# Series of products on constants in row groups, ahead of the first logits of an agent attention and SoLU kernel

## The chip, the cores and the metric

The kernel runs on one core of a Trainium2 chip. The metric is the device time of one execution in microseconds (us); lower is better. The engines are TensorE (PE, with its weight loads shown apart as PEld), VectorE (DVE), ScalarE (ACT), GpSimd (POOL) and SyncE (SP), which here only issues DMAs. Each engine runs its own list of instructions in order; semaphores tie the lists together.

## The reference

Four batches of 12608 tokens with 128 channels go through an attention over 49 agents, and the result through a feed-forward part of width 1024.

```python
def sm(a, b):
    s = scale * (a @ b.transpose(0, 2, 1))
    s = s - s.max(-1, keepdims=True)
    e = np.exp(s)
    return e / (e.sum(-1, keepdims=True) + 1e-09)
agent_v = sm(agents, k) @ v
x = (sm(q, agents) @ agent_v).reshape(B * S, D)

h = x @ w_in
e = np.exp(h - np.max(h, axis=-1, keepdims=True))
solu = h * (e / (np.sum(e, axis=-1, keepdims=True) + 1e-09))
ln = (solu - mean) / np.sqrt(var + 1e-06) * g_ln
out = ln @ w_out
```

## The kernel before

Phase A (`phase_a`) computes `agent_v` for a batch and folds it with `w_in`. The keys come in 12 chunks of 1024 and a tail: logits of a chunk on PE (`p1_mm`, L523, two products of 512 columns into the two halves of the output partitions), a running maximum on DVE (L528, L533 and L535), the exponential on ACT (L549), transposes on PE (`p2_t`, L556), a copy out of PSUM (L567), products with v on PE (`p2_mm`, L577) and their accumulation on DVE (L586). For batch 0, the head of the kernel, the chunks of k and v are loaded ahead into buffers that the later phases use (`kload` L501, `vload` L512, both on SP's queue; the second four slabs of v take the buffers of the first four of k). Beside this DVE, ACT and POOL convert the weights, which arrive as 64-bit numbers, to float32 (`pair_f64`, L368). The head ends with the folded matrices `mh` and `ml` (L648, L653), computed from L641.

Phase B makes the softmax over the agents for 8 tiles of 128 tokens at a time (L767 to L817). Phase C does the feed-forward part of the 396 tiles: L867 (products into the two-bank tiles `ph2`), L871 (maximum), L881 (exponential), L886, L892, then for one half of the tiles transposes on PE (L899) and fp32r products (L982), for the other half a transpose on DVE (L906), DMAs (L916) and float32 products (L922).

The order of all this is set before the kernel runs. `Plan` simulates the engines with costs and due times and emits the instructions in the order in which they would start; at the end each engine's instructions from `marks` (L469) on are tied to that order. What was emitted before `marks`, the constants, is placed by the scheduler where it fits: `ident` (L330, made by POOL), `identR`, its fp32r copy by DVE (L332), `ones` (L334, DVE), and the zeroed `packs` (L453, POOL). Where the plan sees PE idle for over 0.2 us before the head's end, `idle` (L1068) fills in products on `ones` into `ph2[1]` (L1071), 14 of them at the start. They are part of PE's fixed list. The PSUM tiles are `ph2`, two of two banks each, and four banks `px`.

```python
def idle(gap):
    if mlast[0].end is None and gap > 0.2:
        for _ in range(int(0.7 * gap / 0.11) if plan.at["P"] > 2.0 else 14):
            nc.tensor.matmul(ph2[1][:, : 2 * P], warm[:, :P], warm, start=True, stop=True)
```

Of the kernel before, what the change touches and what calls it, by code (L numbers as in the profile page):

```python
# [25 lines left out]
class Plan:  # L26
# [28 lines left out]
    def op(self, eng, fn, cost, due, deps=(), take=False, free=None, after=(), kind=1, shy=0.0):  # L55
        o = Op()
        o.kind, o.shy = kind, shy
        o.eng, o.fn, o.cost, o.due, o.take, o.free = eng, fn, cost, due, take, free
        o.deps, o.outs, o.end, o.bank = [d for d in deps if d is not None], [], None, None
        o.left = 0  # L60
        for d in o.deps + [d for d in after if d is not None]:
            if d.end is None:
                o.left += 1
                d.outs.append(o)
        if not o.left:
            self.push(o)
        return o
# [133 lines left out]
def kernel(  # L201
# [11 lines left out]
    nc = tc.nc  # L213
# [3 lines left out]
    P = 128  # L217
    NF = DF // P
    HW = 512
# [109 lines left out]
    ident = const.tile([P, P], F32, name="ident")  # L329
    make_identity(nc, ident)  # L330
    identR = const.tile([P, P], F32R, name="identR")
    nc.vector.tensor_copy(out=identR, in_=ident)  # L332
    ones = const.tile([P, P], F32, name="ones")
# [116 lines left out]
    packs = []  # L450
# [13 lines left out]
    ph2 = [ps_h.tile([P, DF], F32, name=f"ph{i}") for i in range(2)]  # L464
# [2 lines left out]
    plan.HOLD, plan.STICK = HLD, STK  # L467
    op = plan.op
    marks = len(nc.cur_bb.bb.instructions)  # L469

    TB = NCK * CT + (CKT + P - 1) // P
    seq = [(b, t) for b in range(B) for t in range(TB)]
# [639 lines left out]
    for x in range(n):  # L1112
        b, t = seq[x]
        G, j = slot[x]
        i = x // 2
# [14 lines left out]
        if isY:  # L1130
            TBT[x] = op("D", F(c_tb, x), 1.165, at(x, DTB, DTBR, DTBL), [U[x]] + MV.get(back(G, 2), []))
            if j == GT - 1:
                a = [TBT[2 * z + q] for z in units[G][1] for q in range(2)]
# [4 lines left out]
                for q in range(GT * NF // YC):  # L1138
                    a, k0 = divmod(q * YC, NF)
# [42 lines left out]
        if j == GT - 1:  # L1182
# [21 lines left out]
            else:  # L1204
                o = op("D", d0, 0.6, x + DR, [o, SP[utl[-UTB]]])
                p = op("P", d1, 0.88, x + DR, [o], take=True)
# [71 lines left out]
```

## Time and profile before

| | us |
|---|---|
| time, median of 3 runs | 1471.67 |
| lowest and highest run | 1469.97, 1474.09 |
| span of the profiled execution, first to last instruction | 1472.9 |
| PE busy | 1444.4 |
| DVE busy | 1376.2 |
| ACT busy | 1291.1 |
| POOL busy | 1071.1 |

The profile was taken of one execution of the same program; its span stands within the spread of the runs, 1.2 us above their median, and no other time is given for it. Busy times are sums over an engine's instructions. The matmuls of PE are pipelined, so that one row's duration is longer than the distance to the next one; where a pace is wanted, the starts of neighbours count. A releaser is what ended an idle time, found from the semaphores.

### The profile page before, as it was taken

The numbers are of one execution on the slowest core, as the hardware profiler recorded it, in microseconds if no ns is written. First come the engines' busy times: TensorE is split into PE (matmuls) and PEld (weight loads), VectorE is DVE, ScalarE is ACT, GpSimd is POOL, SyncE is SP. The second block draws the span as 40 slices with busy tenths as digits, with TensorE's granted clock in tenths as the row PEclk, the third lists the DMA queues.
The fourth block names the chain that finished last, engine by engine and source line by source line (L and its number), as shares of the span: only waits on it lengthen the run. The fifth ranks groups of instructions, "written<-read, shape, count | busy, mean of one in ns | idle before, by whom it ended". The sixth has DMA issues, their size and how long they took to land.

```text
span 1472.9 us, 33358 instructions
## 1 busy us (share of the span) xinstructions
PE 1444.4 (98%) x12033; PEld 1279.7 (87%) x12033; DVE 1376.2 (93%) x2024; ACT 1291.1 (88%) x2486; POOL 1071.1 (73%) x1521
## 2 busy tenths in 40 slices
PE   8889999999999999999999999999999999999998
PEld 4668889898888898899898798998999999999998
DVE  5899999999999999999989899999999999999985
ACT  5489999999898998899987898988989999999985
POOL 2485887777776777688677667787768887887854
PEclk9899999999999999999999999999999999999999
DMA  9356565565456756654746666566455455554541
GB/s 369 130 137 194 145 166 149 152 160 142 130 140 187 183 144 160 155 167 114 191 105 159 175 169 175 142 164 166 113 140 135 116 150 131 132 142 106 138 107 44
DMA packets 113253, 221.90 MB, mean 151 GB/s; under 512 B 47552, under 2 KB 50880, under 8 KB 113088
## 3 DMA queue, kind: packets, MB, share of 16 engines
q1 hardware_dynamic: 113088, 219.77, 55.7%
q8 instruction: 95, 1.56, 0.5%
q14 instruction: 70, 0.57, 0.1%
HBM read 92.87 MB, written 26.15 MB: 81 GB/s over the span
## 4 chain that ended last, share of the span: by engine, by line
PE 64%; DVE 15%; ACT 12%; issue 4%; DMA 3%; SPq 2%; POOL 0%; ACTq 0%; DVEq 0%; POOLq 0%
PE ph L867 16%; PE px L922 16%; PE px L982 13%; PE px L899 8%; DVE u L886 5%; ACT e L881 5%; DVE nm L871 4%; ACT uT L952 3%; ACT e L892 3%; PE px L523 3%; DVE tb L906 3%; PE px L577 3%; PE px L767 2%; SPq L916 2%; PE px L812 1%
## 5 line engine op out<-in xcount | busy, mean ns | idle before, releaser
L881 ACT ACTIVATE e<-ph,nm 128x1024 f32<-128x1024 f32 x396 | 443.3, 1123 | 88.1 <-DVE nm L871 84.4
L871 DVE TENSOR_REDUCE nm<-ph 128x1 f32<-128x1024 f32 x396 | 467.2, 1207 | 31.8 <-PE ph L867 29.9
L886 DVE SCALAR_TENSOR_TENSOR u<-ph,e 128x1024 f32<-128x1024 f32 x396 | 471.7, 1218 | 18.7 <-ACT e L881 15.1
L965 POOL TENSOR_TENSOR uL<-uT,uH 128x1024 fp32r<-128x1024 f32 (+1 forms) x198 | 471.3, 2380 | 12.2
L892 ACT ACTIVATE e<-u,su 128x1024 bf16<-128x1024 f32 x396 | 459.1, 1163 | 20.2 <-DVE u L886 19.6
L922 PE MATMUL px<-w,uY 128*128 128x128 f32 x3072 | 375.6, 276 | 0.0
L922 PEld LDWEIGHTS px<-w,uY 128*128 128x128 f32 x3072 | 359.9, 192 | 13.9 <-issue 8.4
L867 PE MATMUL ph<-mh,pT 128*128 128x512 f32 x792 | 335.4, 423 | 7.7 <-DVE u L886 7.3
L867 PE MATMUL ph<-ml,pT 128*128 128x512 f32 x792 | 312.8, 395 | 1.9 <-DVE ml L653 1.9
L961 POOL TENSOR_SCALAR uH<-uT 128x1024 fp32r<-128x1024 f32 (+1 forms) x198 | 207.8, 1049 | 87.0 <-ACT uT L952 87.0
L982 PE MATMUL px<-uH,wH 128*128 128x256 f32 x816 | 237.8, 291 | 0.4 <-ACT eT L567 0.4
L906 DVE STREAM_TRANSPOSE tb<-u 128x1024 f32<-128x1024 f32 x192 | 235.8, 1233 | 0.7
L982 PE MATMUL px<-uH,wL 128*128 128x256 f32 x816 | 228.4, 280 | 0.0
L982 PE MATMUL px<-uL,wH 128*128 128x256 f32 x816 | 228.0, 279 | 0.0
L952 ACT COPY uT<-px 128x512 f32<-128x512 f32 x394 | 213.7, 597 | 11.7 <-PE px L899 11.1
L899 PE MATMUL px<-ident,u 128*128 128x128 f32 x1632 | 218.1, 275 | 1.1 <-ACT uT L952 0.6
L899 PEld LDWEIGHTS px<-ident,u 128*128 128x128 f32 x1632 | 186.2, 142 | 15.8 <-ACT uT L952 3.8
L867 PEld LDWEIGHTS ph<-mh,pT 128*128 128x128 f32 x792 | 150.1, 190 | 39.5 <-DVE u L886 13.4
L867 PEld LDWEIGHTS ph<-ml,pT 128*128 128x128 f32 x792 | 150.7, 190 | 24.4 <-DVE ml L653 2.3
L982 PEld LDWEIGHTS px<-uH,wH 128*128 128x128 f32 x816 | 153.8, 188 | 15.6 <-issue 11.4
L982 PEld LDWEIGHTS px<-uL,wH 128*128 128x128 f32 x816 | 155.2, 190 | 3.7 <-issue 0.5
L982 PEld LDWEIGHTS px<-uH,wL 128*128 128x128 f32 x816 | 153.7, 188 | 0.0
(127 smaller groups left out, 1570.1 us busy)
## 6 DMA issues: line engine op xcount, KB each, us to landing
uY<-tb SPq DMA_DIRECT2D x768, 128.0 KB, 2.6
qt<-in_qT_dram SPq DMA_DIRECT2D x48, 512.0 KB, 4.2
kt<-in_kT_dram SPq DMA_DIRECT2D x36, 512.0 KB, 4.4
vt<-in_v_dram SPq DMA_DIRECT2D x36, 512.0 KB, 4.1
rB<-dr SPq DMA_DIRECT2D x50, 256.0 KB, 4.1
out_dram<-rB SPq DMA_DIRECT2D x50, 256.0 KB, 2.0
out_dram<-oy SPq DMA_DIRECT2D x48, 256.0 KB, 2.7
kh<-in_kT_dram SPq DMA_DIRECT2D x12, 512.0 KB, 8.7
```

The source lines that it names most:

```text
L867: nc.tensor.matmul(ph[:, sl], lhs, bmats[b]["mh" if m == 0 else "ml"][:, sl], start=(m == 0), stop=(m == 1))
L871: nc.vector.tensor_reduce(out=nms[x], in_=phs[x], op=ALU.max, axis=AX.X, negate=True)
L881: nc.scalar.activation(out=es[x], in_=phs[x], func=AF.Exp, bias=nms.pop(x), accum_out=st[G]["S"][:, j : j + 1])
L886: nc.vector.scalar_tensor_tensor(out=u, in0=phs[x], scalar=INV, in1=es[x], op0=ALU.mult, op1=ALU.mult, accum_out=su)
L892: nc.scalar.activation(out=sq, in_=u, func=AF.Square, bias=su, scale=-float(DF), accum_out=st[G]["Q"][:, j : j + 1])
L899: nc.tensor.transpose(pt[:, kf * P : (kf + 1) * P], us[x][0][:, k0 * P : (k0 + 1) * P], ident)
L906: nc.vector.transpose(to, us[x][0].rearrange("p (k r c) -> p k r c", r=GT, c=SQB))
L922: nc.tensor.matmul(st[G]["po"][:, a * P : (a + 1) * P], yb[G][1][:, a, kf].rearrange("p x c -> p (x c)"), w2[:, kf, :], start=(kf == 0), s ...
L952: nc.scalar.copy(out=rr[x][:, hf * 4 : hf * 4 + 4, :], in_=pt)
L961: nc.gpsimd.tensor_scalar(out=uH, in0=rr[x][:, k0:k1, :], scalar1=1.0, scalar2=0.0, op0=ALU.mult, op1=ALU.add)
L965: nc.gpsimd.tensor_tensor(out=uL, in0=rr[x][:, k0:k1, :], in1=uH.bitcast(F32), op=ALU.subtract)
L982: nc.tensor.matmul(po, wt[:, kf, :], ut[:, kf, :], start=(q == 0), stop=(q == WM - 1))
```

## The change

Right after `marks`, and so ahead of everything that the plan emits, PE gets seven series of products. `trial(rows, cols, steps, lhs, rhs)` cuts the 128 partitions into groups of `rows`, and in each of `steps` rounds gives every group one product of `cols` columns: the group's rows of the identity (`ident`, float32, or `identR`, fp32r) as weights and its rows of `ones` (read again for each block of 128 columns) or of the zeros in `packs[0]` as the moving operand. Each group accumulates over the rounds in one of the four banks of `ph2`. Nothing reads the results; the banks are overwritten later. The plan does not know of these products, so the order of everything else stays.

```diff
     marks = len(nc.cur_bb.bb.instructions)
+
+    def banks(q):
+        return ph2[q // 2][:, (q % 2) * HW : (q % 2 + 1) * HW]
+
+    wide = ones.unsqueeze(1)
+    zeros = packs[0].rearrange("p j i a -> p (j i a)")
+
+    def trial(rows, cols, steps, lhs, rhs):
+        m = cols // P
+        for s in range(steps):
+            for g in range(P // rows):
+                sl = slice(g * rows, (g + 1) * rows)
+                nc.tensor.matmul(banks(g)[:, :cols], lhs[sl, :], rhs(sl, m), start=(s == 0), stop=(s == steps - 1))
+
+    one = lambda sl, m: wide[sl].to_broadcast([sl.stop - sl.start, m, P])
+    rnd = lambda sl, m: zeros[sl, : m * P]
+    trial(32, 128, 12, ident, one)
+    trial(32, 256, 6, ident, one)
+    trial(32, 512, 3, ident, one)
+    trial(64, 512, 4, identR, rnd)
+    trial(32, 256, 6, identR, rnd)
+    trial(128, 512, 4, identR, rnd)
+    trial(128, 128, 8, ident, one)
```

## Rows read from the trace of the kernel before

**Rows 1.** The page: span, shares of the chain that ended last.
```profile
span 1472.9 us, 33358 instructions
...
PE 64%; DVE 15%; ACT 12%; issue 4%; DMA 3%; SPq 2%; POOL 0%; ACTq 0%; DVEq 0%; POOLq 0%
```

**Rows 2.** Timeline, 0 to 30 us: start, duration, engine, line, operation, [idle before].
```profile
1.05 3.17 PE L1071 MATMUL ph<-ones 128*128 128x256 bf16 x14 [1.05 <-DVE ones L334]
1.20 0.30 POOL masks.py:199 TENSOR_SCALAR_AFFINE_SELECT ident<-ident 128x128 f32<-128x128 f32 x1
...
1.44 0.99 POOL L453 MEMSET pack<- 128x512 f32 x2
...
5.99 4.29 PE L523 MATMUL px<-kh,ag_sb 128*64 128x512 f32 x12 [1.77 <-DMA kh<-in_kT_dram]
...
8.00 0.69 DVE L528 TENSOR_REDUCE mxp<-px 128x1 f32<-128x512 f32 x1 [7.01 <-PE px L523]
...
10.32 0.22 DVE L332 CAST identR<-ident 128x128 fp32r<-128x128 f32 x1
...
11.19 0.63 PE L556 MATMUL px<-ident,ek 128*128 128x128 f32 x4 [0.36 <-ACT ek L549]
...
11.74 1.08 PE L523 MATMUL px<-kh,ag_sb 128*64 128x512 f32 x4
```

**Rows 3.** Waits, 0 to 70 us: who waited for whom, total us, times, longest.
```profile
PE px L523 <- DMA kh<-in_kT_dram: 1.8, 1, 1.8
```

**Rows 4.** The chain that ended last, 0 to 80 us: start, duration, what.
```profile
17.96 1.01 PE px L523 x4
...
37.62 1.90 PE px L577 x16
...
42.79 1.02 PE px L577 x16
```

**Rows 5.** Timeline of PE, 0 to 60 us, columns as in group 2.
```profile
53.25 1.88 PE L641 MATMUL px<-win_sb,av_dup 128*128 128x512 f32 x4
54.97 1.25 PE L1071 MATMUL ph<-ones 128*128 128x256 bf16 x10
```

**Rows 6.** Instructions of one line (L641, L1071): duration in ns, min/median/max, first and last start.
```profile
L641 PE MATMUL px<-win_sb,av_dup x16: 590/592/697, 53.3 to 1123.4; 128*128 128x512 f32 x16
...
L1071 PE MATMUL ph<-ones x69: 269/273/421, 1.0 to 56.0; 128*128 128x256 bf16 x69
```

**Rows 7.** Timeline of PE in the steady part, 706 to 722 us.
```profile
712.32 0.28 PE L982 MATMUL px<-uH,wH 128*128 128x256 f32 x1
712.44 0.28 PE L982 MATMUL px<-uL,wH 128*128 128x256 f32 x1
...
713.82 1.95 PE L922 MATMUL px<-w,uY 128*128 128x128 f32 x16
715.74 1.53 PE L899 MATMUL px<-ident,u 128*128 128x128 f32 x12
717.02 0.47 PE L867 MATMUL ph<-mh,pT 128*128 128x512 f32 x1
717.33 0.39 PE L867 MATMUL ph<-ml,pT 128*128 128x512 f32 x1
717.56 0.40 PE L867 MATMUL ph<-mh,pT 128*128 128x512 f32 x1
...
719.04 1.14 PE L767 MATMUL px<-ag_sb,qt 128*64 128x49 f32 x32
```

**Rows 8.** Windows: stretch, busy us of each engine, granted clock, DMA share, GB/s.
```profile
0.00:2.00 2.00, 0.95 (x5) 0.71 (x6) 0.17 (x1) 0.00 (x0) 1.44 (x12) 1.00 0.04 6
...
20.00:22.00 2.00, 2.00 (x12) 0.62 (x8) 0.93 (x3) 1.71 (x5) 0.00 (x0) 1.00 1.01 404
...
60.00:70.00 10.00, 8.48 (x54) 6.95 (x53) 8.86 (x14) 7.00 (x13) 4.97 (x8) 0.51 0.18 52
```

**Rows 9.** Timeline of SP's queue, 0 to 62 us: the second four slabs of v.
```profile
24.32 4.56 SPq L512 DMA_DIRECT2D vh<-in_v_dram  x4
```

## The prediction

> **What bounds the kernel now.** I read the page first [rows 1]: the span is 1472.9 us and PE holds 64% of the chain that ended last, in an order that is fixed before the kernel runs. A delay that reaches the steady part is therefore not made up there. What matters is whether a delay at the very start gets that far. The timeline of the first 30 us [rows 2] shows the start: 14 filler products on `ones` from 1.05 us, idle from 4.22 us, and the first logits (L523) at 5.99 us, when the first slab of k lands. The waits confirm it: 1.8 us of PE idle time there ended with that load, and it is the only idle time of PE in the head that a load ended [rows 3]. The chain of the first 80 us [rows 4] then runs on PE alone from 11.19 us until the products with v begin, 1.01 us for the logits of a chunk, passes to DVE, which also converts the weights, and comes back to PE for the products with v. Work is handed from engine to engine there, and each of them runs its list in order; a later L523 makes all of them later.
>
> The median of the runs is 1471.67 us, 1.2 below the span; I work out a delay from the profile and add it to the median.
>
> **The change, part by part.** Nothing is removed. PE gets seven series ahead of its old first instruction. In matmuls: A 48 of 128 columns, B 24 of 256, C 12 of 512 (float32, 32 rows each); D 8 of 512 on 64 rows, E 24 of 256 on 32 rows (fp32r); F 4 of 512 on 128 rows (fp32r); G 8 of 128 on 128 rows (float32). 128 in all. A float32 matmul is two records, an fp32r one is one: a step of 8 matmuls by L922 is a row of 16 [rows 7].
>
> Price of a full-height matmul, from starts of neighbours at the higher clock [rows 5 to 7]. float32, 128 columns: 16 records of L922 fill 713.82 to 715.74, 1.92/16 = 0.120 a record, 0.24 a matmul. float32, 512 columns: L641, 4 records in 1.88 with a last one of about 0.59 gives (1.88 - 0.59)/3 = 0.43 a record, 0.86 a matmul. 256 columns, on the line between: 0.45. fp32r: 0.115 for 256 columns (712.32 to 712.44) and 0.235 for 512 (717.33 to 717.56).
>
> If the row groups took turns: A 11.5, B 10.7, C 10.3, D 1.9, E 2.8, F 0.9, G 1.9, together 40.1 us. No product of the old kernel uses row groups side by side, so their overlap has to be bounded. The nearest rows are pairs in column halves [rows 4]: two matmuls of 512 columns by L523 take 1.01 where two full ones would take 1.72 (factor 1.70), and 8 of 128 columns by L577 take 1.02 where full ones would take 1.92 (1.88). I take 1.75 for a pair and 1.75 x 1.75 = 3.06 for four groups (an estimate). Then A 3.8, B 3.5, C 3.4, D 1.1, E 0.9, F 0.9, G 1.9: 15.5 us. The bounds are 4 and 2 without loss (12.6 us) and no overlap (40.1 us). I take the value near the first because rows of pairs show nearly the full factor, and because each group has rows and a bank of its own, as a column half has columns of its own.
>
> The Trainium skill gives a measured price for just this, in "TensorE: Matmul & The Clock Gate", Part 3: four 32-row products of 512 columns side by side ran 3.07 times as fast. No run of this case shows it yet; by that figure the sum would be the same within 0.1 us.
>
> A change of shape costs a little: L867 after L899 starts its second product 0.31 after the first instead of 0.235 [rows 7], 0.08 more. Five changes at 0.1: 0.5 us; at a full tail (0.27 record against 0.115 pace) they would be 0.8. The skill's "TensorEngine Tiling (Array Packing)", Key Properties, says that a change of the tiling mode drains the engine, which speaks for that second figure: 0.3 us more.
>
> **The clock.** The 14 fillers at 1.05 us took 3.17 us, (3.17 - 0.42)/13 = 0.21 each with a last one of 0.42; the ten at 54.97 us took (1.25 - 0.27)/9 = 0.109 [rows 2, 5, 6]. 256 columns in 0.21 us is 1.2 GHz, in 0.109 it is 2.4 GHz, so the start ran at the lower level although the granted clock is shown as 1.00 there [rows 8]. The first chunk of L523 was still slow (DVE could start on it only 2.01 us later [rows 2] instead of about 1.05), and the first three took 4.29 us instead of 3 x 1.01: 1.26 us too long, so at most 2.5 us of them ran at half pace. PE had been busy for 3.17 and 2.5 us when the level rose. I let the first 5.7 us of the trial run at half pace, which costs 2.9 us; 1.3 us if 2.5 us of unbroken work are enough.
>
> **What hides it.** The trial can't start at 1.05 us: it needs the identity, which POOL ends at 1.20 + 0.30 = 1.50 [rows 2]; I take 1.6. It adds one wait for that on PE's queue, behind which the fillers and all of L523 stand. The copy to `identR` (L332, 10.32 us) moves ahead of L528 on DVE, which is idle until 8.00 us: nothing, or 0.13 us gained. `pack`, the source of zeros, is set from 1.44 us [rows 2], long before series D. The banks are `ph`, next written by the fillers and then by L867 at the head's end, all on PE: no wait. Then the 14 fillers follow, now at the higher clock, 14 x 0.109 = 1.5 us.
>
> The sum: 1.6 + 15.5 + 0.5 + 2.9 + 1.5 = 22.0 us for the first L523, instead of 5.99: 16.0 us later. Given back: its first chunk takes 1.05 instead of 2.01 us, 0.95 us; the second and third slab of k have landed by then, which brings nothing more, since the transposes at 11.19 us wait for DVE and ACT on the first chunk. Delay 16.0 - 0.95 = 15.0 us.
>
> Later cover: the loads of v on SP's queue (24.32 us [rows 9], four slabs that reuse the buffers of k's first four) would wait for the fourth chunk, done at 11.74 + 1.08 = 12.8 us now [rows 2] and at 27.8 then: 3.5 us late, with the tails of v and the last slabs behind them on SP. Their products stand behind 37.62 us on PE [rows 4] and move by 15.0 us too, so this costs nothing; without that cover it would be at most those 3.5 us. Forecast: 1471.67 + 15.0 = 1486.7 us.
>
> **The rivals.**
> *The groups take turns.* 40.1 instead of 15.5: 24.6 us more, 1511.3 us. For it: no row shows row groups side by side. Against it: column halves do overlap without being told to.
>
> *Weights come one load at a time.* Each of A's 96 records needs its own load of 128 columns. L899 has 12 records of 128 columns from 715.74 to 717.02, 0.107 each [rows 7]; that is the pace if loads do not overlap. A 96 x 0.107 = 10.3, B 48 x 0.107 = 5.1, E 24 x 0.107 = 2.6, the rest as before: 25.3, 9.8 us more, 1496.5 us. Against it: the 32 records of L767, with 64 columns of weights each, run at 1.14/32 = 0.036 [rows 7], so loads of two column halves come at twice 0.054 at least. The skill's "TensorE: Matmul & The Clock Gate", LDWEIGHTS, is the rule for this rival: a load of 32 rows takes as long as one of 128 rows, (128 columns)/1.2 = 107 ns. No row of this case shows whether row groups load at once.
>
> *The level of the clock does not rise in the trial.* Then 16.0 us take 32, the fillers 3.0, and the 0.95 us are not given back: 16.0 - 2.9 + 1.5 + 0.95 = 15.5 more, 1502.2 us. For it: 3.17 us of fillers did not raise it. Against it: L523, with halves of the array, did.
>
> *Not slower: the head is bound by its loads.* The DMA engines are busy with a share of 1.01 at 20 us [rows 8]. If PE only follows the loads, a late start is made up and the time stays at 1472 us. It decides where PE's idle time ended by loads reaches 15 us; rows show 1.8 us, and that lies ahead of 5.99 and is already spent [rows 3]. A small ally: the stretch 60 to 70 us has a granted clock of 0.51 [rows 8], and at the higher level its 8.48 busy us would be 4.2 us shorter; even that leaves 11 us.
>
> **How the numbers follow.** Forecast 0.72, turns 0.10, weights 0.08, clock 0.05, not slower 0.05. The forecast's own range: the perfect overlap with the small clock loss gives 15.0 - 2.9 - 1.6 = 10.5; weights that load at L767's 0.036 per 64 columns, 0.072 a record, add 96 x 0.072 - 3.8 + 24 x 0.072 - 0.9 = 3.9, drains 0.3, a slow fetch of instructions about 1: 20.2. So 1482 to 1492, with the spread of the runs (1470.0 to 1474.1) 1480.5 to 1494. To hold 8 in 10 the range reaches on over the weights and the clock, up to 1503. A measurement of this kernel tells 0.3%, 4.4 us, from no change: slower 0.94, within 0.3% 0.04, faster 0.02.
>
> **What would show it.** In the profile of the changed kernel: 220 more PE records, in the 20 us ahead of L523; records of A some 0.039 apart (turns: 0.12; weights: 0.107); the first L523 at 22 us; the first transposes (L556) about 15 us after their old 11.19; the same distance between stages from there to the end. I am wrong if A's records stand 0.1 apart or more, if the fillers behind the trial still take 0.21 each, or if the chain between 22 and 60 us shows loads ending PE's idle time.

## The result and the profile after

The changed kernel takes 1486.04 us (median of 4 runs, 1481.79 to 1488.48) against 1472.88 us of the kernel before in the same comparison: a ratio of 1.0085, 95% interval 1.0059 to 1.0112. It is slower by about 13 us, 0.9%; the forecast was 15.0 us (1486.7).

The profiled execution has a span of 1480.0 us; a time is 1.8 us more than its span in all runs that list both, so this one took 1481.79 us and was the fastest of the four. That matters below: the two profiles differ by 7.1 us, the medians by 13.2. By the same 1.8 us the profiled execution of the kernel before, with its span of 1472.9, took about 1474.7 us: 3 us above the median of its first three runs, and not the 1.2 that a span set beside times suggests. The page of the changed kernel, lines as in [rows 1]:

```profile
span 1480.0 us, 33798 instructions
...
PE 65%; DVE 14%; ACT 11%; issue 4%; DMA 1%; SPq 1%; POOL 0%; ACTq 0%; DVEq 0%; POOLq 0%
```

Its timeline from 0 to 36 us, columns as in [rows 2]; lines of code have moved by 23 (L523 is now L546, L556 is L579, L528 is L551, L1071 is L1094; the trial is L482):

```profile
1.53 1.07 DVE L332 CAST identR<-ident 128x128 fp32r<-128x128 f32 x1 [0.54 <-POOL ident masks.py:199]
...
1.55 9.60 PE L482 MATMUL ph<-ones,ident 32*128 32x128 f32 x168 [1.55 <-POOL ident masks.py:199]
...
11.08 3.26 PE L482 MATMUL ph<-pack,identR 64*128 64x512 f32 x36
...
14.18 1.95 PE L482 MATMUL ph<-ones,ident 128*128 128x128 f32 x16
...
15.96 1.69 PE L1094 MATMUL ph<-ones 128*128 128x256 bf16 x14
...
17.58 2.80 PE L546 MATMUL px<-kh,ag_sb 128*64 128x512 f32 x12
...
18.71 0.69 DVE L551 TENSOR_REDUCE mxp<-px 128x1 f32<-128x512 f32 x1 [16.10 <-PE px L546]
...
21.80 0.66 PE L579 MATMUL px<-ident,ek 128*128 128x128 f32 x4 [0.88 <-ACT ek L572]
```

The three rows of L482 hold series A to C (168 records), D to F (36) and G (16): 220 records, as counted. They run from 1.55 to 15.96 us, 14.4 us. The first logits no longer wait for a load; the 1.77 us of [rows 2, 3] are gone. The first transposes come at 21.80 instead of 11.19 us, 10.6 later. `identR` has moved ahead on DVE, at no cost. Further down, the second group of transposes of phase B, which waits for DVE, has moved by the same 10.6 us; first the kernel before, then the changed one:

```profile
35.59 0.54 PE L812 MATMUL px<-identR,pack 128*128 128x128 f32 x4 [1.75 <-DVE av L586]
```
```profile
46.22 0.54 PE L835 MATMUL px<-identR,pack 128*128 128x128 f32 x4 [1.74 <-DVE av L609]
```

How closely the groups overlap shows in two narrower looks at PE's timeline, 2.4 to 4.2 us and 5 to 5.72 us, both within series A:

```profile
2.14 2.36 PE L482 MATMUL ph<-ones,ident 32*128 32x128 f32 x40
```
```profile
4.81 1.17 PE L482 MATMUL ph<-ones,ident 32*128 32x128 f32 x36
```

The second row is 9 rounds of four groups: with a last record of 0.27 us, (1.17 - 0.27)/8 = 0.112 us for a round, as long as one record of series G on all rows takes ((1.95 - 0.28)/15 = 0.111). Four 32-row products cost what one costs. In the first row a round takes (2.36 - 0.42)/9 = 0.216: the clock's lower level. The trace's first record of the clock, the rise to the full level, stands at 4.68 us (in the kernel before at 9.04).

SP's queue, as in [rows 9], and a stretch in which the loads end:

```profile
29.20 6.23 SPq L535 DMA_DIRECT2D vh<-in_v_dram  x8
```
```profile
44.00:48.00 4.00, 2.19 (x19) 1.65 (x21) 3.88 (x9) 1.78 (x5) 1.31 (x1) 1.00 0.21 84
```

The later slabs of v are issued 4.9 us after their old time, and all loads of the head are still done by about 45 us (DMA share 0.21 here).

### The profile page after: what moved, and what is told of

It is laid out like the page before. It is cut to its first block, busy times and chain, and to the rows that moved or that the text cites. A ratio compares the mean times of both kernels' runs of the same rounds, so it can differ in the third digit from the quotient of the medians.

```text
span 1480.0 us, 33798 instructions
## 1 busy us (share of the span) xinstructions
PE 1452.3 (98%) x12253; PEld 1288.1 (87%) x12253; DVE 1376.4 (93%) x2024; ACT 1290.5 (87%) x2486; POOL 1068.9 (72%) x1521
## 4 chain that ended last, share of the span: by engine, by line
PE 65%; DVE 14%; ACT 11%; issue 4%; DMA 1%; SPq 1%; POOL 0%; ACTq 0%; DVEq 0%; POOLq 0%
PE ph L890 17%; PE px L945 16%; PE px L1005 13%; PE px L922 8%; ACT e L904 5%; DVE u L909 5%; DVE nm L894 4%; ACT uT L975 3%; ACT e L915 3%; DVE tb L929 2%; PE px L790 2%; PE px L600 2%; PE px L546 2%; PE px L835 2%; PE px L579 1%
## 5 line engine op out<-in xcount | busy, mean ns | idle before, releaser
L988 POOL TENSOR_TENSOR uL<-uT,uH 128x1024 fp32r<-128x1024 f32 (+1 forms) x198 | 471.1, 2379 | 12.2
L922 PE MATMUL px<-ident,u 128*128 128x128 f32 x1632 | 217.5, 274 | 1.1 <-ACT uT L975 0.6
L922 PEld LDWEIGHTS px<-ident,u 128*128 128x128 f32 x1632 | 185.5, 141 | 15.8 <-ACT uT L975 3.2
L890 PEld LDWEIGHTS ph<-ml,pT 128*128 128x128 f32 x792 | 150.4, 190 | 24.6 <-DVE ml L676 2.6
```

The source lines that it names most:

```text
L890: nc.tensor.matmul(ph[:, sl], lhs, bmats[b]["mh" if m == 0 else "ml"][:, sl], start=(m == 0), stop=(m == 1))
L922: nc.tensor.transpose(pt[:, kf * P : (kf + 1) * P], us[x][0][:, k0 * P : (k0 + 1) * P], ident)
L988: nc.gpsimd.tensor_tensor(out=uL, in0=rr[x][:, k0:k1, :], in1=uH.bitcast(F32), op=ALU.subtract)
```

## The experiments

Times of the stages from the timelines of all profiles, us; the head from the first transposes on is cut at the second group of transposes of phase B (35.59 us in the kernel before, L812) and at the first exponential of the feed-forward part (61.61 us there, L881). "Runs" is the median, with the ratio to the kernel before in the same comparison.

| kernel | first logits | first transposes | to L812 | to L881 | from there to the end | runs | ratio, 95% interval |
|---|---|---|---|---|---|---|---|
| before, profile above | 5.99 | 11.19 | 24.40 | 26.02 | 1411.3 | 1472.8 to 1474.0 | |
| e5_before | 5.41 | 9.71 | 24.62 | 24.52 | 1410.0 | 1470.53, one run | |
| changed | 17.58 | 21.80 | 24.42 | 24.48 | 1409.3 | 1486.04 | 1.0085, 1.0059 to 1.0112 |
| e1_again | 18.00 | 22.21 | 24.44 | 27.41 | 1410.0 | 1486.25 | 1.0091, 1.0077 to 1.0106 |
| e2_turns | 56.91 | 61.13 | 24.44 | 26.01 | 1412.3 | 1524.70 | 1.0353, 1.0338 to 1.0367 |
| e3_full | 18.30 | 22.61 | 24.41 | 25.97 | 1410.5 | 1485.54 | 1.0087, 1.0072 to 1.0103 |
| e4_twice | 31.48 | 35.70 | 24.44 | 26.00 | 1409.2 | 1497.62 | 1.0173, 1.0157 to 1.0188 |
| e6_start | 6.02 | 10.33 | 24.41 | 25.99 | 1411.9 | 1472.95 | 0.9997, 0.9988 to 1.0006 |
| e7_gaps | 5.83 | 10.13 | 24.43 | 24.49 | 1413.5 | 1475.83 | 1.0020, 1.0011 to 1.0029 |
| e8_fits | 6.67 | 10.89 | 24.42 | 26.04 | 1413.5 | 1473.81 | 0.9999, 0.9989 to 1.0009 |
| e9_two | 6.70 | 11.12 | 24.40 | 24.51 | 1407.8 | 1470.20 | 0.9975, 0.9964 to 0.9985 |
| e10_nofill | 17.35 | 21.57 | 24.43 | 24.53 | 1412.4 | 1484.02 | 1.0068, 1.0056 to 1.0081 |

**The changed kernel again (e1_again).** No edit.

> The changed kernel once more, for its mean and a second profile. In the two profiles the delay is 10.6 us at the first transposes (21.80 against 11.19 us) and 7.1 at the end, while the medians differ by 13.2. Theory 'pure delay, 1:1': the mean difference is 10 to 13 us, and what profiles differ by beyond 10.6 is the time that TensorE spent at the lower clock later on (before: 36.35 to 39.76 and 60.24 to 70.48 us among others). Rival 'partly swallowed': the difference is 7 us in every execution with the same delay at the first transposes.

The difference is 13.4 us (1.0077 to 1.0106 of 1472.8 is 11.3 to 15.6), the first transposes 22.21. So the 7.1 us between the first two profiles are not what the change costs. The table says where they come from: the delay of 10.6 us passes to L812 unchanged (24.40 and 24.42). After that the kernel before takes 1.5 us more in its own profile (26.02 against 24.48), with a stretch of lower clock in that part, and another 2.0 from there to the end. In e1_again it is the changed kernel that loses, 27.41. The stretch of the kernel before, from 36.35 us, and a window of e1_again that holds one of 6.8 us; the column after POOL is the granted clock:

```profile
36.35:39.76 3.41, 3.41 (x24) 2.29 (x23) 3.13 (x8) 1.09 (x4) 1.27 (x1) 0.50 1.04 369
```
```profile
45.00:60.00 15.00, 13.35 (x131) 9.86 (x133) 11.65 (x29) 4.46 (x12) 3.60 (x3) 0.77 0.02 7
```

The five profiles without such a stretch just behind the wait at L812 take 24.5 us from there to L881, the six with 3.4 us of it 26.0, the one with 6.8 us 27.4.

**The kernel before again (e5_before).** No edit.

> The kernel before, once more, for a second profile. Theory 'the profile of before was one of its slower executions by the clock, delay passes 1:1': its span is below 1472.9, its first transposes stand at 10.2 to 11.2 us, and from its own profile to one of the changed kernel the time differs by what the first transposes differ, to 2 us, apart from time at the lower clock. Rival 'swallowed': its first transposes at 11.2 and its end again only 7 us ahead.

PE's timeline of this execution:

```profile
1.05 3.09 PE L1071 MATMUL ph<-ones 128*128 128x256 bf16 x14 [1.05 <-DVE ones L334]
5.41 1.08 PE L523 MATMUL px<-kh,ag_sb 128*64 128x512 f32 x4 [1.26 <-DMA kh<-in_kT_dram]
```

Here the first slab landed 0.6 us earlier and the level rose before L523: its first chunk takes 1.08 us. The first transposes come at 9.71, ahead of the 10.2 to 11.2 that I had expected. Against the changed kernel's two profiles that is 12.1 and 12.5 us, and the ends differ by 11.2 (1480.0 - 1468.8) and 15.3. From the means of the two profiles of each, the delay is 22.0 - 10.45 = 11.6 us at the first transposes and 1482.0 - 1470.9 = 11.2 at the end. The rival of a swallowed delay, 7 us at the end, falls. The strongest number against it comes from e2_turns, the next experiment: against e1_again, in the same comparison, its first transposes are 38.9 us later (61.13 - 22.21) and its time 38.5 us longer (1524.70 - 1486.25).

**The groups one after the other (e2_turns).**

```diff
-        for s in range(steps):
-            for g in range(P // rows):
+        for g in range(P // rows):
+            for s in range(steps):
```

> The same 128 products, but all rounds of one row group before the next group, so that neighbours use the same rows. Theory 'row groups overlap fully': series A, B and C, now without neighbours in other groups, take about four times as long, records 0.11, 0.22 and 0.43 us apart, the trial some 38 us instead of 14.4, and the time is 23 to 27 us above the changed kernel's. Rival 'a product on 32 rows is cheap in itself': trial 14.4 us and time unchanged. Rival 'loads of weights hide only behind another group': records of A 0.2 us apart, trial over 50 us.

```profile
1.55 43.16 PE L482 MATMUL ph<-ones,ident 32*128 32x128 f32 x168 [1.55 <-POOL ident masks.py:199]
44.64 7.46 PE L482 MATMUL ph<-pack,identR 64*128 64x512 f32 x36
51.90 3.56 PE L482 MATMUL ph<-ones,ident 128*128 128x128 f32 x16
55.29 1.69 PE L1094 MATMUL ph<-ones 128*128 128x256 bf16 x14
56.91 2.80 PE L546 MATMUL px<-kh,ag_sb 128*64 128x512 f32 x12
```

The same products take 53.7 us instead of 14.4. Overlap of the groups is shown: at the same lower level a record costs 0.213 us here and a round of four 0.216 in the changed kernel. The turns are not quite strict: around each change of group some records of the two groups start 6 ns apart, which is why series A to C take 43 us and not the 61 of turns throughout. I had expected 38 us for the whole, and 23 to 27 us above the changed kernel in time, which came out as 38.5. The difference is the clock: series G, all rows, takes (3.56 - 0.42)/15 = 0.21 a record, twice its price, and the trace's first record of the clock, the rise, stands at 55.27 us, as G ends (the fillers at 55.29 run at 0.11). The third rival, loads that hide behind other groups only, would have given such times too; the pace of G and the record of the clock speak against it, since G is the same in both kernels and a record on one group costs no more at this level than one on all rows. The products with v did not idle although SP's queue waited 33.7 us for the logits to give up the buffers of k: 24.44 us to L812 as ever.

**Full-height fillers of the same length (e3_full).**

```diff
-    trial(32, 128, 12, ident, one)
...
-    trial(128, 128, 8, ident, one)
+    for _ in range(120):
+        nc.tensor.matmul(ph2[1][:, : 2 * P], warm0[:, :P], warm0, start=True, stop=True)
```

> In place of the trial 120 fillers (bf16, 256 columns, all 128 rows): at 0.21 us each up to about 4.7 us, then 0.109, they end at about 16 us, as the trial does. Theory 'only the length counts': first transposes at 21.5 to 22 us and the same time as the changed kernel within 3 us. Rival 'row groups cost something of their own (drains, clock)': the time differs by more, or the clock rises at another point than 3.1 us after the first product.

```profile
1.05 15.79 PE L488 MATMUL ph<-ones 128*128 128x256 bf16 x120 [1.05 <-DVE ones L334]
16.68 1.69 PE L1090 MATMUL ph<-ones 128*128 128x256 bf16 x14
18.30 2.79 PE L542 MATMUL px<-kh,ag_sb 128*64 128x512 f32 x12
```

Ratio 1.0087 against 1.0091 of the changed kernel, with intervals that nearly coincide: what the products are makes no difference that these runs can show; how long they hold PE does. The first transposes came at 22.61, later than expected, because the clock rose 5.2 us after the first product (at 6.25). By the letter that is the rival's sign; but with row groups the rise comes anywhere from 3.1 to 5.9 us after it (five profiles), so it does not tell the two apart.

**The trial twice (e4_twice).** All seven calls in `for _ in range(2):`.

> All seven series twice. The second pass runs at the higher clock: 12.8 us. Theory 'pure delay, 1:1': first transposes at 34.6 us and the time 12.8 us above the changed kernel's, 23 to 26 us above before. Rival 'partly swallowed in the proportion of the profiles, 7.1 of 10.6': 8.6 us more. Rival 'SP's queue comes into play': the second four slabs of v wait for the fourth chunk of k, some 11 us more than in the changed kernel, and the products with v idle for loads.

```profile
1.56 10.50 PE L482 MATMUL ph<-ones,ident 32*128 32x128 f32 x168 [1.56 <-POOL ident masks.py:199]
11.99 3.25 PE L482 MATMUL ph<-pack,identR 64*128 64x512 f32 x36
15.07 10.00 PE L482 MATMUL ph<-ones,ident 128*128 128x128 f32 x184
25.01 3.24 PE L482 MATMUL ph<-pack,identR 64*128 64x512 f32 x36
28.08 1.95 PE L482 MATMUL ph<-ones,ident 128*128 128x128 f32 x16
29.86 1.69 PE L1095 MATMUL ph<-ones 128*128 128x256 bf16 x14
```

The second pass begins 16 records of G after 15.07, at 16.95, and ends at 29.86: 12.9 us, the price at the higher level. The first transposes came at 35.70 instead of the expected 34.6: in this execution the first pass, with its stretch at the lower level, took 15.4 us and not 14.4. The runs are 11.4 us above the changed kernel, nearer to 12.9 than to 8.6; the edges of the two intervals leave 7.5 to 16.3, so by itself this is weak. The distance to L812 is 24.44: SP's queue made nothing wait.

**A trial that fits ahead of the load (e8_fits).** Series A alone, and no fillers at the start:

```diff
-            for _ in range(int(0.7 * gap / 0.11) if plan.at["P"] > 2.0 else 14):
+            for _ in range(int(0.7 * gap / 0.11) if plan.at["P"] > 2.0 else 0):
```

> The kernel before with series A alone (48 products of 128 columns in four groups of 32 rows) in place of the 14 fillers at the start. A took 4.26 to 5.17 us in three executions, from 1.55 us, so it ends at 5.8 to 6.7. Theory 'only what outlasts the first load counts': first L523 at 6.0 to 6.8 us, first transposes at 10.2 to 11 us, time within 2 us of before. Rival 'row groups ahead of the logits cost in themselves': time 5 us or more above before.

```profile
1.55 5.19 PE L482 MATMUL ph<-ones,ident 32*128 32x128 f32 x96 [1.55 <-POOL ident masks.py:199]
6.67 2.80 PE L540 MATMUL px<-kh,ag_sb 128*64 128x512 f32 x12
```

Ratio 0.9999 (0.9989 to 1.0009): row groups in place of the fillers cost nothing measurable where PE would have waited for the first slab.

**Without the fillers behind the trial (e10_nofill).** The edit of e8_fits in the changed kernel.

> The changed kernel without the 14 fillers behind the trial. They take 1.6 us there. Theory 'pure delay, 1:1': first L523 at 16.0 to 16.4 us, first transposes at 20.2 to 20.6, time 1.6 us below the changed kernel's median of 1486, so 1483 to 1486. Rival 'the fillers keep the clock up for the logits': the clock falls before the first transposes and nothing is gained.

The median is 2.0 us below the changed kernel's; by the ratios of the two comparisons (1.0068 against 1.0091, whose intervals overlap) it is 3.4. Both agree with the 1.6 us, and neither measures it. The first transposes came at 21.57, outside the expected 20.2 to 20.6, because the trial took 15.8 us in this execution (1.55 to 17.35), 2.9 more than at the higher level throughout: the clock rose at 7.43 us. It stayed up until 68.87, so the rival of a clock that falls without the fillers is out for this execution.

**More fillers at the start (e6_start).** 26 instead of 14 in the line above, in the kernel before.

> The kernel before with 26 instead of 14 fillers at the start, so that TensorE is busy until the first slab of k lands at about 6 us. Theory 'work that ends before the load costs nothing and the clock rises earlier': the clock rises between 4.7 and 6.6 us instead of 9.04, the first transposes come at about 10.2 instead of 11.2, time 0 to 1.5 us below before. Rival 'the fillers of the start delay': first L523 after 6.4 us, time up to 1 us above before.

The clock rose at 5.24 us, the first transposes came at 10.33, as expected, and the time is unchanged (0.9997, 0.9988 to 1.0006). The start varies by more than that between executions of the kernel before (11.19 and 9.71).

**Fillers in the waits of the head (e7_gaps, e9_two).** With the idle stretches of PE as the suspected cause of the clock's falls, fillers were put into them: in e7_gaps into six waits, of which four needed a bank of `px`, in e9_two only into the two that could use `ph2[1]`; both have 26 fillers at the start.

```diff
+            if (k, q) == (0, 1):
+                fill(ph2[1], 13)
...
+            if (x, hf, m) == (0, 1, 1):
+                fill(ph2[1], 14)
```

> The kernel before with 26 fillers at the start and with fillers in the waits of TensorE in the head: 13 ahead of the transposes at 35.59 us, 14 ahead of the product at 58.80, and 10, 8, 17 and 11 ahead of tiles 2, 5, 6 and 8, each shorter at 0.109 us than the wait (1.74, 1.88, 1.52, 1.21, 2.29, 1.58 us). Theory 'the idle gaps of the head let the clock fall, and that costs 2 to 6 us': no stretch at the lower clock between 30 and 90 us and a time 3 to 6 us below before. Rival 'the stretches cost nothing, since DVE ends the head': the clock stays up and the time is that of before within 1.5 us.

> The kernel before with 26 fillers at the start, 13 ahead of the transposes at 35.59 us and 14 ahead of the product at 58.80, all into a bank that nothing reads then; none of the fillers ahead of tiles 2, 5, 6 and 8, which in the run before waited for their PSUM bank (2.6 and 2.8 us). Theory 'the two long waits of the head make the clock fall, and that costs time': no stretch at the lower clock between 30 and 60 us, the first maximum of the feed-forward part 1 to 3 us earlier, time 1 to 3 us below before. Rival 'the waits for DVE that follow end at the same time': clock up, time that of before within 1 us.

e7_gaps is slower, 1.0020, against 3 to 6 us faster in the expectation. Two of the fillers in `px` waited themselves for a bank to be read out, and PE with them; the clock was not kept up either, with the lower level from 75.77 to 82.60 and from 89.43 to 92.84 us:

```profile
77.55 3.78 PE L867 MATMUL px<-ones 128*128 128x256 bf16 x17 [2.62 <-ACT pT L819]
...
88.11 1.36 PE L867 MATMUL px<-ones 128*128 128x256 bf16 x11 [2.77 <-ACT uT L965]
```

e9_two beats both kernels: 1470.20 us against 1474.04 in its comparison, ratio 0.9975 (0.9964 to 0.9985), more than the 1 to 3 us expected. Its fillers end inside the waits, and the windows that held lower stretches in the kernel before (0.89 and 0.66 for 30 to 45 and 60 to 75 us in the profile above) are at 1.00:

```profile
33.61 1.58 PE L866 MATMUL ph<-ones 128*128 128x256 bf16 x13
35.52 0.54 PE L814 MATMUL px<-identR,pack 128*128 128x128 f32 x4 [0.33 <-DVE av L586]
```
```profile
30.00:45.00 15.00, 14.45 (x173) 11.03 (x168) 14.71 (x35) 6.22 (x19) 6.72 (x8) 1.00 1.01 382
45.00:60.00 15.00, 14.31 (x162) 10.18 (x156) 13.89 (x24) 2.33 (x5) 10.42 (x9) 1.00 0.24 76
60.00:75.00 15.00, 9.50 (x72) 6.56 (x72) 15.00 (x21) 12.54 (x23) 9.39 (x13) 1.00 0.18 42
```

That the clock is what brings the gain is supported by the runs, which list a granted clock of 0.995 to 0.999 against 0.990 to 0.996 of the kernel before; three profiles without these fillers (e5_before, the changed kernel, e10_nofill) had no fall just behind L812 either, so one profile could not show it. Products of no use help here because they stand in front of an instruction that waits anyway; the trial of the change stands in front of one that would have run.

## Why the prediction was right, and where its steps were not

The mechanism was the forecast one: a pure delay of PE ahead of L523 that nothing later makes up. The distance from the first transposes to L812 is 24.4 us in eleven profiles and 24.6 in one, whether the delay is 0, 11, 25 or 50 us; the rival of a head bound by loads is out. Step by step:

- The start of the trial was right: 1.55 us for 1.6.
- The products were mis-sized: 15.5 + 0.5 us for them and their changes of shape, against 12.9 in the second pass of e4_twice. The step that failed is the factor 1.75 x 1.75 for four groups. It is 4: a round takes 0.112 us, one record on all rows 0.111. The bound of the forecast without loss (12.6 us) was close to the truth. The Trainium skill's 3.07, in "TensorE: Matmul & The Clock Gate", Part 3, stood as near to my factor and as far from the measurement.
- The reading behind that factor failed first. Pairs in column halves lose nothing either: the six pairs of the row at 17.58 us start (2.80 - 0.59)/5 = 0.44 us apart, where one record on all columns takes 0.43; the 16 records by L577 that [rows 4] shows at 42.79 start in pairs that follow, after the first, 0.103 us apart, where one record on all columns takes 0.11. The 1.01 and 1.02 us of [rows 4] run from one kind of product to the next, so they hold the changes of shape at both ends (0.05 behind the first pair of a chunk by L546 and 0.10 behind its last). The forecast took this cost for a loss of overlap, carried it over to four groups as a square, and then added 0.5 us for changes of shape on top. The 0.120 us a record of L922 holds one such change too; inside the row it is 0.112.
- The changes of shape cost more than the 0.5 taken: at the paces of the series the products sum to 2.70 + 2.60 + 2.58 + 0.94 + 0.68 + 0.94 + 1.78 = 12.2 us, so 0.7 of the 12.9 are changes. The starts in that pass tell where: C to D, D to E and E to F, where the number of rows changes, cost 0.2 us each, and 0.1 lies in the first round, behind the 128 rows of G; A to B, B to C and F to G, where only columns or type change, cost less than 0.01. The Trainium skill's "TensorEngine Tiling (Array Packing)", Key Properties, says that a change of the tiling mode drains the engine, and not a change of tile. The trace agrees: 0.2 us a change is nearer to the 0.16 of the prediction's larger figure (0.8 for five) than to its 0.1.
- The clock was somewhat mis-sized: 2.9 us forecast, 14.4 - 12.9 = 1.5 in the first profile, 14.8 - 12.9 = 1.9 in e1_again, 2.5 in the first pass of e4_twice and 2.9 in e10_nofill. It varies between executions, over nearly all of the stretch between the 1.3 and the 2.9 of the forecast. The record of the clock puts the rise in the kernel before at 9.04 us, 3.05 us after L523 began, where I had read at most 2.5.
- The fillers behind the trial took 15.96 to 17.58, 1.62 us for 1.5. The given-back part was right: from first logits to first transposes 4.22 instead of 5.20 us, 0.98 for 0.95.
- SP's queue behaved as described: the second four slabs were issued 4.9 us late, for 3.5, and cost nothing.
- The upper end of the range held about 1 us for a slow fetch of instructions. No run shows such a term: apart from the first round and the changes of rows, the 220 records of the trial follow each other at their paces.

The sum of these gives 10.6 us at the first transposes of the profiled execution, not 15.0, and yet the medians differ by 13.2 and 13.4. Part of the rest is the base: the profile of the kernel before, on which the sum was made, is one in which the level rose late and the first transposes came at 11.19 us; in its other profile they came at 9.71. Against the two the delay is 10.6 to 12.5 us. So the sum put the first transposes at 26.2 us, 4 us later than they came (21.80 and 22.21), while the difference of the medians is only 1.6 to 1.8 us under the forecast 15.0. (That 1486.04 stands within 0.7 of 1486.7 comes from the median of the kernel before, which rose by 1.2 with a fourth run.) That the time was hit so closely is luck. Of the sum's error, 0.7 us is made up by the base (11.19 against 10.45, the mean of the two profiles of before). The rest lies between 11.6, the mean delay of the profiles, and the 13.2 and 13.4 of the medians. The two profiled executions of the changed kernel took 1481.79 and 1485.91 us, on average 2 us below its medians, those of before about 1474.7 and 1470.53, on average at theirs, so the profiles are too few to show it; 11.6 also lies inside the interval of 11.3 to 15.6. Where the slower executions of the changed kernel lose their time stays open; whether the changed kernel also meets more stretches of the lower clock later (its runs list a granted clock of 0.990 to 0.995, those of before 0.994 to 0.997 in the comparison of e1_again) isn't settled by two profiles of each.

The rivals: groups in turn is refuted by e2_turns, loads of weights one at a time by the 0.112 us of a round. The clock that does not rise was wrong for the change (4.68 us in its first profile) and came true only in e2_turns. All groups in one bank was not tried.

## What to carry to other kernels

Work put ahead of a fixed order costs its own length less the wait that it fills: 0 for 5.2 us of products that end with the first load, 13 us for 16 us that don't. Before a sum is made on one profile, look at a second one for stretches at the lower clock, here worth 1.5 us for each 3.4 us just behind the wait at L812. A price read from one row to the next of another kind holds the change between them: take the pace from starts inside a row. And fillers can pay where PE waits for another engine and a free bank is at hand: two such places gave 3.8 us, while with four more, in banks of `px`, two of which waited to be read out, the kernel was slower than without any.

## What the hardware showed beyond that

- Four 32-row groups with a bank each run at four times the rate of one: 0.112 us for a round of float32 records of 128 columns and, between 6.5 and 8.1 us, (2.11 - 0.37)/8 = 0.217 for 256 columns. Two 64-row groups of fp32r with 512 columns start 3 ns apart and rounds follow at 0.235 us.
- In e2_turns the clock stayed at its lower level through 43 us of products on nearly always one 32-row group at a time; it rose at 55.27 us, after 5.2 us of products on all rows (series F and G). With four groups side by side it rose 3.1 to 5.9 us after the first product (five profiles), with full-height products without a pause 3.0 to 5.9 (e3_full, e6_start, e7_gaps, e9_two).
- The granted clock is shown as 1.00 from 0 us in every window although the pace is that of the lower level; the trace has no record before the first change, the rise (between 3.93 and 9.04 us, in e2_turns at 55.27), so the level of the start is read from paces.
